# A decode block's backward pass: some weight loads and gradient stores move from SyncE's DMA queue to GpSimd's

## The chip, the cores and the metric

The kernel runs on one core of one Trainium2 chip. The metric is device time in microseconds (us) of one execution; the figure for a kernel is the median over several. A core has five engines with a queue of instructions each: TensorE (PE, with its weight loads shown apart as PEld), VectorE (DVE), ScalarE (ACT), GpSimd (POOL) and SyncE (SP). Memory traffic is carried by 16 DMA engines, which the profile shows by queue and packet. Any of SP, ACT and POOL can issue a DMA; the instruction that does so stands in that engine's own queue, in order with its other work.

## The reference, cut to what matters

One decode step (one token, batch 2) through attention and a gated MLP side by side, and then the gradients of everything. The forward part is

```
xn  = layernorm(x)                                  # x: 2 x 1 x 576
q   = xn @ wq                                       # wq: 576 x 4096, 32 heads of 128
p   = softmax(q k^T / sqrt(128));  o = p v          # k, v: 2 x 16 x 4096 x 128, two q heads share one kv head
out = x + o @ wo + ((xn @ w_gate) * (xn @ w_up)) @ w_down   # wo: 4096 x 576; F = 4608
```

and what is returned is `out` and the gradients for x, the k cache, the v cache, wq, wo, w_gate, w_up and w_down, all in bf16. The gradients of the caches are as large as the caches, those of the weights as large as the weights. With one token for each of two batch rows every weight gradient is an outer product of rank 2, and every cache gradient one of rank 2 (two q heads). So nearly every byte is either read once or written once: 92.48 MB in, 92.48 MB out.

## The kernel before, in words

**Tiles and stages.** Attention is worked in 16 steps (s): 8 groups g of two kv heads, and for each the two batch rows. A step loads two K tiles and two V tiles of 1 MB (128 partitions x 8 KB, `load_kv`, L1044), turns each by 32x32 blocks on VectorE (`turn`, L1113), makes scores on TensorE (`score`, L1162), the softmax (`softmax`, L1211), contracts with V and K (`contract`, L1335), and writes two dK and two dV tiles of 1 MB as outer products (`head_outer`, L1183), which go through PSUM, are copied to a `big` buffer by ScalarE or VectorE (`cp`, L461 and L463) and stored. The blocks `BD` that the outer products need are built by GpSimd, 3.6 us each (`build_BD`, L1150); so are the small stationaries `W` (`build_W`, L1127) and `wt` (`stationaries`, L661).

A group has a front (`group_front`: q from wq, the gradient of o from wo) and a back (`group_back`, L957: the gradients of that group's 512 columns of wq and 512 rows of wo, its share of the output and of dx). The MLP runs in 9 slices of 512 columns (`mlp`) between the steps.

**What is loaded and stored for a group.** `load_w` (L1050) loads a group's wq as 128 partitions x 4 runs of 1,024 bytes (L1063, 512 KB), with two small loads of 32 KB for the last 64 rows (L1059), and wo as 128 partitions x 4 runs of 1,152 bytes (L1068, 576 KB). The four runs of a partition lie together in SBUF and apart in memory. In `group_back` the gradient of wo goes out as 4,608-byte runs (`rows_outer`, 576 KB), the main part of wq's gradient as 1,024-byte runs (`cols_outer` with `cols_store`, L732, 512 KB), and the last 64 rows of wq's gradient as one 64 KB store (`tail_outer`, L759, buffer `tl`). The MLP's weights and gradients use the same helpers with runs of 2,048 bytes.

**What sets the order.** Each piece of work is a generator. A planner written out in the kernel (`Order`, L105) runs them when the program is built: each request has an engine, a cost, and a priority from tables (`PR`, `HEAD`, `TAIL`, `OFF`, with a step of 28 a step); the planner keeps a model of when engines and buffers come free and of two DMA lines (`Lines`, L53), one for SP and ACT and one for POOL, and emits instructions in the order it arrives at. On the chip each engine then runs its own instructions in exactly that order. A DMA is costed at L291: a packet of `row` bytes takes 0.0364 ns a byte and 8.7 ns more. `SLACK` says how far ahead of the earliest candidate an engine may look for one of higher priority. `load_ws` (L1097) holds each weight load until so many cache loads have been issued (`MLP_AT`, `WQ_AT`, `WO_AT`).

**Queues.** In this kernel all loads and stores are issued by SP, but for the two loads of x and grad_out (ACT). `put` (L677) is the one helper for stores: it waits for the copies that fill the buffer and issues on SP. POOL issues no DMA.

The functions that the change touches, and what calls them:

Of the kernel before, what the change touches and what calls it, by code (L numbers as in the profile page):

```python
# [13 lines left out]
P = 128  # L14
# [276 lines left out]
def DMA(engine, cost, nbytes, row=8192):  # L291
    packet = 0.0364 * row + 8.7
    return ("dma", engine, cost, 0.02 + nbytes / 16e3 * packet / row, packet)
# [2 lines left out]

NBIG, NGU, NWW, NBD = 16, 1, 6, 3
CAP = {"kv": 7, "X": 12, "st": 4, "G": 2}
OFF = {"mload": {0: -36.3, 1: 16.8, 2: -19.8, 3: -330.5, 5: 42.4, 6: -111.1, 7: -82.2, 9: 191.7, 10: -151.2,
       11: 244.5, 13: -16.7, 15: -5.8}, "wload": {0: 329.7, 1: -827.0, 2: -91.1, 3: 193.0, 4: -575.9, 5: 77.0,  # L300
       6: -97.7, 7: 317.9, 8: 179.1, 10: 110.7, 11: 107.3, 12: 101.9, 13: 558.1, 14: -92.8, 15: 306.7},
       "BD1": {0: 482.2, 1: -53.2, 2: -3.3, 3: 120.6, 4: -601.2, 5: -133.1, 6: 127.1, 7: -234.1, 8: -45.0, 9: 65.6,
       10: 99.4, 12: -193.8, 13: 284.9, 14: -109.9, 15: 42.6}, "out1": {0: 49.6, 1: 283.1, 2: 49.7, 3: -222.7,
       5: 323.4, 6: 229.4, 7: -322.6, 8: 142.3, 9: 293.7, 10: 4.2, 11: 63.5, 12: -219.7, 13: -100.2, 14: 383.8,
       15: 47.0}, "W1": {0: -170.8, 1: -216.4, 2: -400.0, 3: -75.8, 4: -98.4, 5: 118.6, 6: 303.1, 7: 8.0, 9: 60.0,
       10: -3.6, 11: -275.6, 12: -452.3, 13: 182.8, 14: -7.3, 15: 237.8}, "turn1": {0: -195.1, 1: -56.4, 2: -119.7,
       3: 124.4, 4: 468.7, 6: -73.7, 7: 79.5, 8: -132.5, 9: -229.3, 10: -53.9, 11: 85.0, 12: 1.5, 14: -33.0,
       15: 38.8}, "load": {0: 38.1, 1: -50.7, 2: 166.0, 4: -99.4, 5: -145.2, 6: -9.7, 7: 192.6, 8: -2.7, 9: 97.8,
       10: -119.3, 12: 290.3, 13: -19.5, 14: -128.7, 15: 181.9}, "front": {0: 9.1, 1: 170.2, 2: 128.1, 3: 372.2,
       4: 357.2, 5: -384.9, 6: -177.7, 7: -129.0, 8: 13.5, 9: 71.0, 10: 224.9, 11: 9.5, 12: -117.9, 13: -9.4,  # L310
       14: -468.5, 15: -30.4}, "turn0": {0: -455.2, 1: -90.8, 2: 0.2, 3: 28.7, 4: -0.9, 5: -231.7, 6: 2.8, 7: 67.0,
       8: -476.7, 9: 30.4, 10: -61.0, 11: 29.9, 12: 6.4, 13: -275.6, 14: 105.2, 15: 86.1}, "con": {0: 60.0, 1: 31.3,
       2: 117.9, 3: -65.0, 4: 446.2, 5: 4.0, 6: -193.2, 7: -1.9, 8: 27.1, 9: -358.4, 10: 38.5, 11: -215.9, 12: -87.1,
       13: 7.6, 15: 22.9}, "W0": {0: -4.4, 1: 75.7, 2: -298.1, 3: 59.6, 4: 289.8, 5: -179.5, 6: 58.5, 7: -263.0,
       8: -20.6, 9: 21.9, 12: 520.5, 13: -109.7, 14: -223.2, 15: -36.8}, "back": {0: -320.5, 1: 0.4, 2: 125.7,
       3: 144.8, 4: -34.1, 5: 27.8, 6: -144.7, 7: -3.0, 8: -92.9, 9: -20.3, 10: -85.3, 11: -52.0, 13: 82.4,
       14: -138.2}, "BD0": {0: 13.0, 1: -92.4, 2: 161.5, 3: -159.8, 4: -155.8, 6: -113.5, 7: -55.4, 9: 148.4,
       10: 97.8, 11: 7.0, 12: -22.3, 13: 117.7, 14: 473.8, 15: 16.2}, "out0": {0: -47.5, 1: -241.0, 2: 70.9,
       3: -176.7, 4: -156.5, 5: -403.1, 7: 101.3, 8: -9.1, 9: -258.5, 10: 100.0, 11: -93.4, 12: 255.6, 13: -226.2,
       14: -11.9, 15: -60.8}, "dsc": {0: -366.7, 2: 10.9, 3: 185.9, 5: -2.6, 7: 31.8, 8: -250.0, 9: 24.5, 10: 26.4,  # L320
       12: -2.1, 13: -284.2, 14: 187.2, 15: -38.2}, "mlp": {0: -345.4, 2: 692.3, 3: -3.8, 4: -34.2, 5: 612.9,
       6: 368.1, 7: -119.8, 8: 31.4, 10: -111.7, 11: -100.0, 12: 51.0, 13: 219.8, 14: 9.4, 15: 136.1},
       "att": {0: -32.2, 1: 181.3, 2: 325.2, 3: 101.2, 4: 36.6, 5: 184.0, 6: -133.3, 7: -37.0, 8: 57.4, 9: 139.5,
       10: -6.1, 11: -267.5, 12: 36.3, 13: -80.2, 14: -101.6}, "conv": {0: -191.0, 1: -570.3, 2: 91.8, 3: 215.3,
       4: 4.9, 5: 4.5, 6: 46.9, 7: -237.0, 8: 83.3, 9: -6.7, 10: -56.4, 11: -31.6, 13: -155.6, 14: -88.6, 15: -378.3}}
MLP_AT = [2.38, 3.44, 16.76, 17.06, 29.05, 44.32, 47.73, 43.88, 59.6]
WQ_AT = [-3, 9, 17, 23, 32, 39, 50, 55]
WO_AT = [2, 7, 5, 25, 36, 39, 37, 57]
LATENCY, DRY = {"SP": 0.5, "ACT": 0.5, "POOL": 0.57}, 0.4
LM, LAG = 0.15, 1.75  # L330
CLK = 2.0
BIAS = 0.547
SLACK = {"PE": 0.08, "ACT": 0.3, "DVE": 0.46, "POOL": 24.94, "SP": 1554.58}
STEP = 28.0
HEAD = {"turn0": 358.0, "turn1": -88.8, "att": -420.1, "dsc": 372.9, "con": 241.2, "out1": -625.8, "out0": 80.7,
        "front": 43.6, "back": 73.0, "W0": 584.4, "W1": -340.9, "BD1": 39.3, "BD0": 397.4, "conv": 284.3,
        "load": 102.5}
TAIL = {"turn0": 773.4, "turn1": 743.4, "att": -103.0, "dsc": 772.1, "con": 784.6, "conv": 1032.9, "out1": 1117.1,
        "out0": 440.4, "front": -1213.5, "back": 298.4, "W1": 286.6, "BD1": 566.8, "BD0": -240.2, "load": 315.8,
        "W0": 700.2}  # L340
PR = {"turn0": 179.4, "turn1": -212.5, "att": -999.3, "dsc": -1293.8, "conv": 102.1, "con": -320.2, "out1": 2170.9,
      "out0": 547.6, "front": 160.8, "back": -141.3, "W0": -800.5, "W1": -140.0, "BD1": 814.6, "BD0": -99.0,
      "mlp": -127.6, "wout": -665.8, "store": 229.4, "load": 79.4, "wload": -1000.4, "fin": -292.2, "const": 321.0,
      "mload": -108.2}


def pr(name, s):
# [5 lines left out]
def kernel(  # L353
# [22 lines left out]
    nc = tc.nc  # L376
# [297 lines left out]
                                 rhs=view(Xt, 0, P, toff(q, s), [[2, 32]]),  # L674
                                 start=(s == 0), stop=(s == St - 1))

    def put(dst, src, nbytes, row, tag, slot, ready):  # L677
        yield WAIT(*ready)
        for d, x in zip(dst, src):
            yield DMA("SP", 0.36, nbytes, row)  # L680
            nc.sync.dma_start(d, x)
        yield ("lrel", tag, slot)

    def unit(mms, pe, cols, ev, done, quad=None, kind="r"):
# [44 lines left out]
        yield WAIT(*done)  # L729
        yield SET(event)  # L730

    def cols_store(i, dst, width, done):  # L732
        return put([dst.rearrange("(c p) n -> p c n", p=P)], [st_t[i][:, 0:4 * width].rearrange("p (c n) -> p c n", n=width)],
                   128 * 4 * width * 2, 2 * width, "st", i, done)

    def cols_outer(rhs, dst, p, event):
        i = yield ACQ("st")
        done = events(2)
        yield SPAWN(cols_store(i, dst, FS, done), p + PR["store"])
        for A in range(2):  # L740
            yield SPAWN(unit(*cols_unit(A, rhs, st_t[i]), done[A]), p)
        yield WAIT(*done)
        yield SET(event)
# [12 lines left out]
        yield WAIT(*done)  # L756
        yield SET(event)

    def tail_outer(rhss, dsts, p, event):  # L759
        i = yield ACQ("tl")  # L760
        st = tl_t[i]
        nw, done = len(rhss), events(2)
        yield SPAWN(put(dsts, [st[64 * w:64 * w + 64, 0:FS] for w in range(nw)], 64 * FS * 2, 1024, "tl", i, done),
                    p + PR["store"])

        def mk(A):
            def mms(o):
                for w, rhs in enumerate(rhss):
                    for aa in range(2):
                        a = 2 * A + aa  # L770
                        nc.tensor.matmul(o[64 * w:64 * w + 64, aa, 0:P], lhsT=xnr[32 * a:32 * a + 32, 512:576],
                                         rhs=rhs(a), start=True, stop=True)

            def ev(e, o):
                cp(e, st[0:64 * nw, 256 * A:256 * A + 256].rearrange("p (a f) -> p a f", a=2), o[0:64 * nw, :, 0:P])
            return mms, (0.053, 0.104), 256, ev
        for A in range(2):
            yield SPAWN(unit(*mk(A), done[A]), p)
        yield WAIT(*done)
        yield SET(event)  # L780
# [176 lines left out]
    def group_back(g):  # L957
# [16 lines left out]
        po = pr("back", 2 * g) + PR["wout"]  # L974
        yield SPAWN(rows_outer(R[:], out_5[n0:n0 + FS, :], po, E[0]), po)
        yield SPAWN(cols_outer(lambda a: R[32 * a:32 * a + 32, 1, :], out_4[0:512, n0:n0 + FS], po, E[1]), po)
        yield SPAWN(tail_outer([lambda a: R[32 * a:32 * a + 32, 1, :]], [out_4[512:576, n0:n0 + FS]], po, E[2]), po)
        m = yield ACQ("m")
        yp = m_t[m][:, 0:10].rearrange("p (k b) -> p k b", b=2)
        yield PE(0.0, 0.52)  # L980
# [69 lines left out]
    def load_w(item):  # L1050
        kind, i = item
        if kind in ("wq", "wo"):
# [3 lines left out]
            if kind == "wq":  # L1056
                for h in range(2):
# [1 line left out]
                    nc.sync.dma_start(ww_t[w][64 * h:64 * h + 64, 4 * FS:WB],  # L1059
                                      A_wq[512:576, n0 + 256 * h:n0 + 256 * h + 256])  # L1060
                yield ("lset", st["Lq"])
                yield DMA("SP", 0.4, 128 * 4 * FS * 2, 1024)
                nc.sync.dma_start(ww_t[w][:, 0:4 * FS].rearrange("p (c n) -> p c n", n=FS),  # L1063
                                    A_wq[0:512, n0:n0 + FS].rearrange("(c p) n -> p c n", p=P))
                yield ("lset", st["Lm"])
            else:
                yield DMA("SP", 0.4, 128 * GH * D * 2, 1152)
                nc.sync.dma_start(ww_t[w][:, 0:GH * D].rearrange("p (h n) -> p h n", h=GH),  # L1068
                                  A_wo[n0:n0 + FS, :].rearrange("(h p) n -> p h n", p=P))
                yield ("lset", st["Lo"])  # L1070
        else:
# [419 lines left out]
```

## Time and profile before

| | |
|---|---|
| median of 3 runs | 482.09 us (481.51 to 482.98) |
| the profiled execution's own time | 483.47 us |
| its span, first to last instruction | 481.7 us (1.8 us lie around it) |
| mean granted TensorE clock | 0.675 |
| busy: PE, PEld, DVE, ACT, POOL | 386.8, 217.9, 360.0, 343.2, 155.4 us |
| moved by DMA | 185.94 MB, mean 386 GB/s |

How to read it: busy times are of the engine itself; time in which its queue waits or issues a DMA is not counted. The page's second part cuts the span into 40 slices of 12 us, each digit a busy share in tenths; the row "DMA" is the mean busy share of the 16 DMA engines, and "GB/s" what they moved. A DMA answer for a short window counts the packets that start in it, by size class, and gives the time those packets took as a share of 16 engines over the window; packets run over the window's end, and so a full second can show a little over 100%. A packet here is one run of bytes (1,024, 1,152, 2,048, 4,608 or 8,192) or a 4-byte completion. The DMA instruction lasts only as long as its issue; "us to landing" is counted from there to the arrival of its data.

### The profile page before, as it was taken

What the parts mean: (1) busy time and instruction counts of PE and PEld (TensorE: products, weight loads), DVE (VectorE), ACT (ScalarE), POOL (GpSimd) and SP (SyncE); (2) the same over time, 40 slices, a digit from 0 to 9 for tenths busy, and PEclk for the clock granted to TensorE, in tenths of its full rate; (3) what the DMA queues carried; (4) which work ended last, traced back from release to release, by engine and by line L of the source; (5) the groups of instructions that cost most, each with busy time, mean ns of one, the idle gap of its engine ahead of it and who ended that gap; (6) DMA issues with size and microseconds to landing.
All of it is one profiled execution on the core that took longest, in us unless ns stands there. A gap on an engine that the chain in (4) does not pass through costs nothing.

```text
span 481.7 us, 15312 instructions
## 1 busy us (share of the span) xinstructions
PE 386.8 (80%) x6530; PEld 217.9 (45%) x6530; DVE 360.0 (75%) x667; ACT 343.2 (71%) x520; POOL 155.4 (32%) x220
## 2 busy tenths in 40 slices
PE   1479699858788878868977899857698899899897
PEld 1456345435444444434654345324465434554444
DVE  8688877867377977776677778866665988788872
ACT  6066578956787596755598779856578877868883
POOL 3110553443011374320026364361102724074100
PEclk9995657669656578677786557756965555765765
DMA  7997999999999999999999999999999999999994
GB/s 289 353 406 269 367 387 386 401 343 399 424 406 417 390 416 420 365 399 407 415 406 417 342 407 422 424 403 388 413 386 411 420 326 403 419 395 419 405 412 163
DMA packets 49652, 185.94 MB, mean 386 GB/s; under 512 B 4008, under 2 KB 21168, under 8 KB 33200
## 3 DMA queue, kind: packets, MB, share of 16 engines
q1 hardware_dynamic: 49576, 184.96, 98.0%
q8 instruction: 51, 0.84, 0.7%
q14 instruction: 17, 0.14, 0.1%
q10 hardware_dynamic: 8, 0.00, 0.0%
HBM read 92.48 MB, written 92.48 MB: 384 GB/s over the span
## 4 chain that ended last, share of the span: by engine, by line
DMA 46%; PE 30%; ACT 10%; DVE 7%; issue 4%; SPq 3%; DVEq 0%; ACTq 0%
DMA out_dram<-big 29%; ACT big L461 8%; PE ps_o L1183 6%; PE ps_m L1335 5%; DMA big<-in_A_k_cache_dram 5%; DMA big<-in_A_v_cache_dram 5%; PE ps_m L1162 4%; DVE big L457 3%; DMA ww<-in_B_w_down_dram 3%; PE ps_o L715 3%; DMA ww<-in_A_wo_dram 2%; PE ps_m L941 2%; DVE big L463 2%; DMA ww<-in_A_wq_dram 1%; PE ps_o L701 1%
## 5 line engine op out<-in xcount | busy, mean ns | idle before, releaser
L461 ACT CAST big<-ps_o 128x1024 bf16<-128x1024 f32 (+1 forms) x319 | 283.0, 955 | 41.0 <-PE ps_o L1183 22.1
L457 DVE STREAM_TRANSPOSE big<-big 128x1024 f32<-128x1024 f32 x146 | 175.8, 1223 | 23.9 <-DMA out_dram<-big 17.0
L1150 POOL TENSOR_TENSOR BD<-vr,mask 128x2048 bf16<-128x2048 bf16 x32 | 115.3, 3602 | 114.1 <-PE ps_o L1183 40.8
L463 DVE CAST big<-ps_o 128x1024 bf16<-128x1024 f32 (+1 forms) x57 | 66.4, 1166 | 12.8 <-PE ps_o L1183 4.3
L1162 PE MATMUL ps_m<-big,W 128*32 128x128 bf16 x2048 | 60.4, 286 | 4.2 <-POOL W L1127 1.3
L1162 PEld LDWEIGHTS <-W 128*32 128x32 bf16 x2048 | 47.8, 127 | 22.4 <-issue 19.3
L1183 PE MATMUL ps_o<-BD,dd 32*128 32x512 bf16 x256 | 51.4, 527 | 7.5 <-ACT big L461 5.5
L1183 PE MATMUL ps_o<-BD,pp 32*128 32x512 bf16 x256 | 47.6, 520 | 8.4 <-ACT big L461 6.4
L1127 POOL COPY W<-rep 32x16 bf16<-32x16 bf16 x128 | 24.5, 192 | 69.9 <-DVE rep L925 65.0
L661 POOL COPY wt<-wm 64x128 bf16<-64x128 bf16 (+1 forms) x34 | 8.9, 261 | 99.2 <-DVE wm L654 98.3
L457 DVE STREAM_TRANSPOSE big<-ww 128x1152 f32<-128x1152 f32 x25 | 34.1, 1365 | 7.5 <-DMA out_dram<-big 4.8
L1335 PE MATMUL ps_m<-big,dd 128*32 128x512 bf16 x256 | 28.8, 540 | 9.8 <-DVE dd L457 4.7
L1335 PE MATMUL ps_m<-big,pp 128*32 128x512 bf16 x256 | 30.2, 566 | 1.4 <-DVE pp L457 0.9
L1183 PEld LDWEIGHTS <-dd 32*128 32x128 bf16 x256 | 12.0, 98 | 30.6 <-issue 26.5
L1183 PEld LDWEIGHTS <-pp 32*128 32x128 bf16 x256 | 11.0, 98 | 24.7 <-issue 21.1
L701 PEld LDWEIGHTS <-xnr 32*128 32x128 bf16 x416 | 13.7, 110 | 14.4 <-issue 12.9
L715 PE MATMUL ps_o<-dyr,R 32*32 32x288 bf16 x256 | 18.1, 396 | 2.1 <-ACT big L461 1.1
L461 ACT CAST osb<-ps_m 128x512 bf16<-128x512 f32 x16 | 9.6, 598 | 12.7 <-PE ps_m L1335 9.3
L941 PE MATMUL ps_m<-big,Wdy 128*128 128x128 bf16 x144 | 15.4, 292 | 3.4 <-DVE cr L1287 1.8
L701 PE MATMUL ps_o<-hb,xnr 32*128 32x128 bf16 x288 | 14.3, 250 | 4.5 <-ACT big L461 3.2
L715 PE MATMUL ps_o<-dyr,hb 32*32 32x288 bf16 x288 | 16.1, 337 | 1.1 <-DVE tl L463 0.5
L941 PEld LDWEIGHTS <-Wdy 128*128 128x128 bf16 x144 | 13.8, 134 | 6.3 <-issue 6.3
(198 smaller groups left out, 486.6 us busy)
## 6 DMA issues: line engine op xcount, KB each, us to landing
out_dram<-big SPq DMA_DIRECT2D x72, 1024.0 KB, 12.2
big<-in_A_k_cache_dram SPq DMA_DIRECT2D x32, 1024.0 KB, 11.5
big<-in_A_v_cache_dram SPq DMA_DIRECT2D x32, 1024.0 KB, 13.1
out_dram<-big SPq DMA_DIRECT2D x17, 576.0 KB, 10.8
ww<-in_B_w_down_dram SPq DMA_DIRECT2D x9, 576.0 KB, 12.4
out_dram<-big SPq DMA_DIRECT2D x10, 512.0 KB, 9.6
ww<-in_A_wo_dram SPq DMA_DIRECT2D x8, 576.0 KB, 12.3
ww<-in_A_wq_dram SPq DMA_DIRECT2D x8, 512.0 KB, 9.7
```

Of the source, the lines that this page charges most:

```text
L457: nc.vector.transpose(out, in_)
L461: nc.scalar.copy(out, in_)
L463: nc.vector.tensor_copy(out=out, in_=in_)
L661: nc.gpsimd.tensor_copy(view(Wt[:], 64 * h, 64, 0, [[dims[-1][1], n], [1, dims[-1][1]]]), view(Wm[:], 64 * h, 64, off, dims))
L701: nc.tensor.matmul(o[:, aa, dc * P:(dc + 1) * P], lhsT=xnr[32 * a:32 * a + 32, dc * P:(dc + 1) * P], rhs=rhs(a), start=True, stop=True)
L715: nc.tensor.matmul(o[32 * q:32 * q + 32, aa, 0:HD2], lhsT=view(t, 32 * q, 32, 2 * A + aa, [[4, 32]]), rhs=dyr[32 * q:32 * q + 32, k * HD2: ...
L941: nc.tensor.matmul(dp, lhsT=Wdy[:, e, 2 * k:2 * k + P], rhs=view(X[:], 0, P, 64 * k + e, [[D, GH], [2, 32]]), start=(k == 0 and e == 0), s ...
L1127: nc.gpsimd.tensor_copy(view(W_t[t][w][:], 32 * a, 32, 6 + 8 * a, [[G * WW, 4], [WW, G], [1, 2]]), view(rep_t[grp[g]["qs"]][:], 32 * a, 32 ...
L1150: nc.gpsimd.tensor_tensor(BD_t[i][:], view(vr_t[v][:], 0, P, 0, [[0, 16], [1, Dh]]), view(mask16[:], 0, P, 0, [[1, 16], [0, Dh]]), ALU.mult)
L1162: nc.tensor.matmul(sc[32 * cq:32 * cq + 32, :], lhsT=view(W[:], 0, P, (be * G + l) * WW + 6 - 4 * c2 - 2 * l, [[1, 32]]), rhs=view(X[:], 0 ...
L1183: nc.tensor.matmul(o[:, k, :], lhsT=pr2[32 * c4:32 * c4 + 32, :], rhs=BD[32 * c4:32 * c4 + 32, 8 * l + 4 * h2:8 * l + 4 * h2 + 4, :], star ...
L1335: nc.tensor.matmul(ct[32 * j:32 * j + 32, :], lhsT=view(rT, 0, P, 4 * c + 2 * l, [[1, 32]]), rhs=kv_t[kvS[s][t][l]][:, Dh * c:Dh * (c + 4) ...
```

## The change

What it does: (1) `put` and `cols_store` get an `engine` argument; with "POOL" the DMA is issued by GpSimd. (2) `cols_outer`, which stores the main part of wq's gradient, uses it: 8 stores of 512 KB. (3) In `load_w`, from the second group on, the main load of wq (7 of 512 KB) and the load of wo (7 of 576 KB) are issued by GpSimd. In the planner's books these 22 DMAs cost the issuing engine 0.78 us (0.36 or 0.4 on SP) and count as rows of 4,096 or 4,608 bytes, four times as long as before. (4) `tail_outer` gets `w0`: the 64 rows of a group's wq tail use partitions 0 to 63 for even groups and 64 to 127 for odd ones. (5) All tables of the planner have other values: the priorities, the gates, two landing delays, the bias between ACT and DVE for copies, and `SLACK`. No arithmetic is added or removed.

```
-MLP_AT = [2.38, 3.44, 16.76, 17.06, 29.05, 44.32, 47.73, 43.88, 59.6]
-WQ_AT = [-3, 9, 17, 23, 32, 39, 50, 55]
-WO_AT = [2, 7, 5, 25, 36, 39, 37, 57]
+MLP_AT = [2.82, 10.88, 15.0, 36.18, 28.54, 28.05, 46.37, 36.8, 60.65]
+WQ_AT = [-6, 9, 17, 24, 32, 29, 48, 55]
+WO_AT = [2, -2, -17, 15, 35, 39, 40, 53]
...
-LM, LAG = 0.15, 1.75
+LM, LAG = 1.27, 1.14
...
-BIAS = 0.547
-SLACK = {"PE": 0.08, "ACT": 0.3, "DVE": 0.46, "POOL": 24.94, "SP": 1554.58}
+BIAS = 0.599
+SLACK = {"PE": 0.04, "ACT": 0.27, "DVE": 0.45, "POOL": 1.44, "SP": 13.16}
...
-    def put(dst, src, nbytes, row, tag, slot, ready):
+    def put(dst, src, nbytes, row, tag, slot, ready, engine="SP"):
         yield WAIT(*ready)
         for d, x in zip(dst, src):
-            yield DMA("SP", 0.36, nbytes, row)
-            nc.sync.dma_start(d, x)
+            yield DMA(engine, 0.36 if engine == "SP" else 0.78, nbytes, row)
+            (nc.sync if engine == "SP" else nc.gpsimd).dma_start(d, x)
...
-    def cols_store(i, dst, width, done):
+    def cols_store(i, dst, width, done, engine="SP"):
...
-                   128 * 4 * width * 2, 2 * width, "st", i, done)
+                   128 * 4 * width * 2, 2 * width if engine == "SP" else 8 * width, "st", i, done, engine)
...
-        yield SPAWN(cols_store(i, dst, FS, done), p + PR["store"])
+        yield SPAWN(cols_store(i, dst, FS, done, "POOL"), p + PR["store"])
...
-    def tail_outer(rhss, dsts, p, event):
+    def tail_outer(rhss, dsts, p, event, w0=0):
...
-        yield SPAWN(put(dsts, [st[64 * w:64 * w + 64, 0:FS] for w in range(nw)], 64 * FS * 2, 1024, "tl", i, done),
+        yield SPAWN(put(dsts, [st[64 * w:64 * w + 64, 0:FS] for w in range(w0, w0 + nw)], 64 * FS * 2, 1024, "tl", i, done),
...
-        yield SPAWN(tail_outer([lambda a: R[32 * a:32 * a + 32, 1, :]], [out_4[512:576, n0:n0 + FS]], po, E[2]), po)
+        yield SPAWN(tail_outer([lambda a: R[32 * a:32 * a + 32, 1, :]], [out_4[512:576, n0:n0 + FS]], po, E[2], g % 2), po)
...
-                yield DMA("SP", 0.4, 128 * 4 * FS * 2, 1024)
-                nc.sync.dma_start(ww_t[w][:, 0:4 * FS].rearrange("p (c n) -> p c n", n=FS),
+                yield DMA("POOL", 0.78, 128 * 4 * FS * 2, 4096) if i else DMA("SP", 0.4, 128 * 4 * FS * 2, 1024)
+                (nc.gpsimd if i else nc.sync).dma_start(ww_t[w][:, 0:4 * FS].rearrange("p (c n) -> p c n", n=FS),
...
-                yield DMA("SP", 0.4, 128 * GH * D * 2, 1152)
-                nc.sync.dma_start(ww_t[w][:, 0:GH * D].rearrange("p (h n) -> p h n", h=GH),
+                yield DMA("POOL", 0.78, 128 * GH * D * 2, 4608) if i else DMA("SP", 0.4, 128 * GH * D * 2, 1152)
+                (nc.gpsimd if i else nc.sync).dma_start(ww_t[w][:, 0:GH * D].rearrange("p (h n) -> p h n", h=GH),
```

## The prediction

> **What bounds the kernel now.** I read the page's first three parts first. Its busy row, DMA row and queue table:
>
> ```profile
> PE 386.8 (80%) x6530; PEld 217.9 (45%) x6530; DVE 360.0 (75%) x667; ACT 343.2 (71%) x520; POOL 155.4 (32%) x220
> ...
> DMA  7997999999999999999999999999999999999994
> ...
> DMA packets 49652, 185.94 MB, mean 386 GB/s; under 512 B 4008, under 2 KB 21168, under 8 KB 33200
> ...
> q1 hardware_dynamic: 49576, 184.96, 98.0%
> ```
>
> No compute engine is over 80% busy, while the packets of one DMA queue, q1 (SP's), take 98.0% of the time of all 16 DMA engines. Under 90% the DMA row shows only the first slice, the fourth and the last. So the time is that of the packets, plus the little in which the DMA engines starve. The chain of waits says the same: 46% of it are DMA, and PE comes only second.
>
> Next I asked for the stages, cut where the DMA row dips (columns: window and its length; busy time of PE, PEld, DVE, ACT, POOL; granted clock; DMA share; GB/s):
>
> ```profile
> 0.00:4.00 4.00, 0.00 (x0) 0.00 (x0) 3.10 (x10) 2.35 (x5) 3.39 (x17) 1.00 0.21 50
> 34.00:41.00 7.00, 5.89 (x131) 3.63 (x128) 6.99 (x14) 3.56 (x5) 0.29 (x1) 0.57 0.54 172
> 41.00:386.00 345.00, 280.56 (x4849) 158.46 (x4847) 256.02 (x446) 254.29 (x387) 122.86 (x155) 0.66 1.02 399
> 386.00:393.00 7.00, 6.39 (x80) 2.29 (x69) 5.88 (x12) 5.31 (x9) 1.76 (x1) 0.50 0.84 307
> 470.00:481.70 11.70, 8.23 (x87) 4.94 (x84) 3.23 (x13) 3.76 (x6) 0.00 (x0) 0.50 0.41 155
> ```
>
> For 345 us on end the DMA engines are full. They starve for 4.0 x 0.79 = 3.2 us at the start, 7.0 x 0.46 = 3.2 us at 34 to 41 us (the first gradients aren't ready and the cache buffers are all taken), 7.0 x 0.16 = 1.1 us at 386 to 393, and 11.7 x 0.59 = 6.9 us at the end. A full DMA engine that moves 399 GB/s where windows of 8 KB packets alone move 426 loses to small packets. What one packet of a kind costs I took from DMA answers for windows that hold almost one kind only. The two most used here, of 1,024 bytes (456 to 457 us) and 8,192 bytes (236 to 240 us):
>
> ```profile
> DMA packets 349, 0.38 MB, mean 381 GB/s; under 512 B 12, under 2 KB 342, under 8 KB 346
> q1 hardware_dynamic: 349, 0.38, 106.7%
> ```
>
> ```profile
> DMA packets 228, 1.70 MB, mean 426 GB/s; under 512 B 20, under 2 KB 20, under 8 KB 20
> q1 hardware_dynamic: 228, 1.70, 100.9%
> ```
>
> The second: 208 packets in 1.009 x 16 x 4 = 64.6 us, 310 ns each. The first: 106.7% of 16 engine-microseconds are 17.1; 4 packets of 2 to 8 KB and 3 of 8 KB take about 1.7, and 15.4 us for 330 packets is 46.7 ns each. In the same way 1,152 bytes (13 to 14 us: 106.3%, 327 packets and one of 8 KB) come to 51.0 ns, 2,048 bytes (47 to 50 us: 104.5%, 588) to 85.3, 4,608 bytes (23 to 24 us: 99.8%, 88) to 181. Per kilobyte the short ones cost 46, the long ones 39 to 40 ns.
>
> **The change, part by part. The packets.** 15 transfers of 512 KB (7 loads of wq, 8 stores of its gradient) are 7,680 runs of 1,024 bytes, 7 of 576 KB (wo) are 3,584 runs of 1,152. The diff counts them as rows of 4,096 and 4,608 bytes, that is, one packet for the four runs of a partition. No row shows a packet of GpSimd's queue, so I bound it. Dear end: packets stay as they are, nothing saved (the bytes and runs are the same, so the engines have no more to carry). Cheap end: the diff's rows are true. A 4,096-byte packet lies between the 2,048 and 4,608 rows at 85.3 + (181 - 85.3) x 0.8 = 162 ns; four short ones are 187. 1,920 times 25 ns over 16 engines: 3.0 us. For wo, four at 51.0 are 204 against 181; 896 times 23 ns over 16: 1.3 us. Together **-4.3 us**. All of it is on the path, since the DMA engines are full in the stages where these transfers lie. I take the cheap end: four runs that lie together in a partition's SBUF are the only thing that sets these transfers apart, and the 4,608-byte row shows that an engine takes such a length as one packet.
>
> The Trainium skill ("DMA: Bandwidth & Descriptors", section "Why small descriptors are slow") puts a packet's fixed cost at about 3 cycles and says that joining is worth it only up to 256 bytes. By its 3 cycles at 850 MHz, 3.5 ns, I estimate 2,816 x 3 x 3.5 / 16 = 1.8 us in place of 4.3. The rows above disagree: 46.7 ns against a fourth of 162, 40.5, is 6 ns a run. The sum stays with the rows.
>
> **SP's queue** loses 22 issues of about 0.5 us (medians of the two load lines: 0.58 and 0.48), 11 us in all, and the waits for the eight gradient stores' copies. SP isn't the bound, since its DMAs take 8 to 15 us to land in a full queue: nothing. What was queued behind those waits, cache loads above all, can go out sooner; it joins a full line.
>
> **GpSimd's queue** gains 22 issues and eight waits for copies. No row shows the price of an issue there: at SP's 0.58 us it is 13 us, at GpSimd's own longest instruction, 3.6 us, it is 79, on 155.4 busy of 481.7. I take 0.58, the same transfer's row. The cover is GpSimd's slack: its BD blocks, asked by line, held up PE for 0.3 us and its weight loads for 0.5 in the whole run. At 79 us each issue would delay a BD block by about one block, once in 22 us; the DMA engines would notice only if stores then ran dry, which is the second rival.
>
> ```profile
> L1150 POOL TENSOR_TENSOR BD<-vr,mask x32: 3601/3602/3605, 49.1 to 443.5; 128x2048 bf16<-128x2048 bf16 x32
> ```
>
> The BD line by source (min, median, max ns) shows GpSimd's longest work undisturbed by a VectorE that is 75% busy: 4 ns between fastest and slowest of 32. That bears on a rule against this change. The Trainium skill ("SBUF — State Buffer", the box on VectorE blocking DMA) says that GpSimd writes the descriptors of its DMAs itself and is locked out while VectorE runs a two-port copy; a 620 ns transfer then took 3,100. By that I estimate 22 x 2.5 = 55 us more on GpSimd, which lies within the two ends above; no run here shows a descriptor being written.
>
> **The tails** move the same 26 stores of 64 KB, with the same packets, from other partitions: nothing. If the half mattered, eight stores of 64 packets at 46.7 ns over 16 engines are 1.5 us in all, and a part of that could be won or lost.
>
> **The tables** change the order everywhere. That moves starving, not packets: at best the stretch at 34 to 41 us closes (-3.2 us; the start and the last step's chain have nothing to load or store), at worst new ones open (second rival). I take nothing.
>
> **Sum:** 483.47 - 4.3 = 479.2 us on the profiled execution's clock. That execution is 1.4 us over the median of 482.09; so 482.09 - 4.3 = **477.8 us**. With the 34 to 41 us stretch closed it is 474.6; with half the saving, about 480.
>
> **Rivals.** *No saving.* GpSimd's queue makes the same packets, and everything else was hidden anyway: 482.1 us. For it: only the diff's own numbers say that runs are joined. The Trainium skill ("DMA: Bandwidth & Descriptors", section "Issuing engines are not separate DMA queues") has this rule: whichever engine issues, the same 16 engines carry it, and only issue time is saved. The first half the trace can't show with one queue; by it alone the time stays. Against it: the change of packet length, which that rule doesn't speak of.
>
> *GpSimd's queue blocks, and the DMA engines starve.* On GpSimd a load or store stands in order behind waits, and BD blocks stand behind its own waits. The waits by engine:
>
> ```profile
> POOL wt L661 <- DVE wm L654: 98.3, 16, 21.1
> POOL W L1127 <- DVE rep L925: 65.0, 14, 15.9
> POOL BD L1150 <- PE ps_o L1183: 40.8, 6, 11.2
> ```
>
> (us in all, times, longest.) A wo load behind a wait of 11 to 21 us lands late; the group's front then waits, and after it scores, outer products and stores. Against it: loads wait for a gate long before they are needed, and wq and wo held up their users for 4.0 and 1.3 us in all. It costs nothing until stores in flight run out; then one starving is worth what 34 to 41 us shows, 3.2 us. Two undo the gain, so it decides from the second on. I price three, in seven groups: 482.1 - 4.3 + 9.7 = **487.5 us**, slower.
>
> **How the numbers follow.** Forecast 0.56; no saving 0.14; blocking 0.30. About 0.3%, 1.4 us, is what a measurement of this kernel can tell from no change. So faster 0.56, same 0.14, slower 0.30. The likeliest case's own range is 474.6 to 480.5. The range must also take in the no-saving case and most of the blocking one: 474.6 to 487.5 us.
>
> **What would show it.** A second queue in the queue table with 7.9 + 4.1 = 12.0 MB, 2,816 packets of 4 KB and more beside its completions, and q1 short of 11,264 packets: "under 2 KB" falls from 21,168 to about 9,900. If the second queue shows 11,264 packets, the first rival holds. The DMA share in the middle stage stays at 1.0 and GB/s rises from 399 by some 4. If GpSimd blocks, PE's waits for BD rise from 0.3 us to tens, and the DMA row shows new digits under 9. GpSimd's issues by line give their price; over 3.6 us my cover is wrong. The forecast fails if two queues at once slow each other's packets: 8 KB packets would then take more than 310 ns while GpSimd's transfers are in flight.

## The result, and the profile after

| | time, us | ratio to before, 95% interval |
|---|---|---|
| before | 482.83, median of 15 runs (481.51 to 484.66) | |
| after | 484.72, median of 15 runs (482.78 to 487.91) | 1.0052 (1.0030 to 1.0074) |

The change makes the kernel slower by 0.5%, where 1% faster was forecast. The profiled execution of after took 487.82 us, 3.1 over its median, span 485.8. From its page: busy row, DMA row, packets, and the queue table (packets, MB, share of 16 engines' time):

```profile
PE 383.6 (79%) x6530; PEld 218.8 (45%) x6530; DVE 353.4 (73%) x661; ACT 348.2 (72%) x526; POOL 172.6 (36%) x242
...
DMA  7997999999999999999999999999999999999994
...
DMA packets 41204, 185.94 MB, mean 383 GB/s; under 512 B 4008, under 2 KB 9904, under 8 KB 24752
...
q1 hardware_dynamic: 37960, 172.97, 90.8%
q0 software_dynamic: 3168, 11.99, 6.5%
```

The marks that the forecast named for the packets are there. A second queue, q0, carries 11.99 MB in 3,168 packets: 352 completions and 2,816 packets of 4 KB and more, so the four runs of a partition are one packet. "Under 2 KB" falls from 21,168 to 9,904. The two queues together take 97.3% of the engines' time where one took 98.0%. The mark for the rate is missing: in the long full stretch (columns as in the prediction; DMA share and GB/s last) the engines move 398 GB/s, where before moved 399 and some 4 more were forecast.

```profile
88.00:428.00 340.00, 279.60 (x4736) 157.19 (x4724) 251.06 (x443) 260.22 (x394) 137.87 (x178) 0.66 1.01 398
```

So the packets changed as forecast and the time didn't follow.

GpSimd's new issues, by line (the store, the wq load, the wo load; ns min, median, max):

```profile
L682 POOL DMA_DIRECT2D out_dram<-big x8: 759/800/800, 86.1 to 477.6; - x8
```

```profile
L1065 POOL DMA_DIRECT2D ww<-in_A_wq_dram x7: 751/792/920, 53.8 to 387.5; - x7
L1070 POOL DMA_DIRECT2D ww<-in_A_wo_dram x7: 751/751/792, 54.8 to 388.3; - x7
```

0.75 to 0.92 us each, 17 us in all, which is the rise of POOL's busy time from 155.4 to 172.6: on GpSimd, unlike on SP, the profile counts an issue as busy. PE waited for BD blocks 1.1 us in the whole run (0.3 before): GpSimd was not short of time.

### The profile page after: what moved, and what is told of

Same layout as the page of the kernel before. It is cut to its first block, busy times and chain, and to the rows that moved or that the text cites. A ratio compares the mean times of both kernels' runs of the same rounds, so it can differ in the third digit from the quotient of the medians.

```text
span 485.8 us, 15354 instructions
## 1 busy us (share of the span) xinstructions
PE 383.6 (79%) x6530; PEld 218.8 (45%) x6530; DVE 353.4 (73%) x661; ACT 348.2 (72%) x526; POOL 172.6 (36%) x242
## 3 DMA queue, kind: packets, MB, share of 16 engines
q0 software_dynamic: 3168, 11.99, 6.5%
## 4 chain that ended last, share of the span: by engine, by line
DMA 40%; PE 32%; ACT 12%; DVE 10%; issue 3%; POOL 1%; SPq 0%; DVEq 0%; ACTq 0%; POOLq 0%
DMA out_dram<-big 22%; ACT big L462 10%; DMA big<-in_B_w_gate_dram 6%; PE ps_o L1185 5%; PE ps_o L716 5%; DVE big L458 5%; DMA big<-in_A_v_cache_dram 5%; PE ps_m L1337 4%; PE ps_m L1164 4%; DMA gu<-in_B_w_up_dram 3%; PE ps_m L943 2%; DMA ww<-in_A_wq_dram 2%; DMA big<-in_A_k_cache_dram 2%; DVE big L464 2%; PE ps_o L702 2%
## 5 line engine op out<-in xcount | busy, mean ns | idle before, releaser
L462 ACT CAST big<-ps_o 128x1024 bf16<-128x1024 f32 (+1 forms) x324 | 287.5, 952 | 43.8 <-PE ps_o L1185 27.2
L464 DVE CAST big<-ps_o 128x1024 bf16<-128x1024 f32 (+1 forms) x52 | 60.7, 1170 | 10.3 <-PE ps_o L1185 3.5
L1185 PE MATMUL ps_o<-BD,pp 32*128 32x512 bf16 x256 | 50.3, 521 | 10.8 <-ACT big L462 8.4
L1185 PE MATMUL ps_o<-BD,dd 32*128 32x512 bf16 x256 | 45.5, 491 | 8.6 <-ACT big L462 5.4
L1337 PE MATMUL ps_m<-big,pp 128*32 128x512 bf16 x256 | 31.7, 583 | 3.6 <-DVE pp L458 2.5
L1337 PE MATMUL ps_m<-big,dd 128*32 128x512 bf16 x256 | 26.8, 510 | 1.7 <-DVE oT L1357 1.4
L1185 PEld LDWEIGHTS <-dd 32*128 32x128 bf16 x256 | 10.7, 97 | 29.3 <-issue 24.5
L716 PE MATMUL ps_o<-dyr,hb 32*32 32x288 bf16 x288 | 18.8, 383 | 3.6 <-DVE tl L464 3.0
L716 PE MATMUL ps_o<-dyr,R 32*32 32x288 bf16 x256 | 19.2, 431 | 1.4 <-ACT big L462 1.4
L462 ACT CAST osb<-ps_m 128x512 bf16<-128x512 f32 x16 | 9.4, 589 | 13.1 <-PE ps_m L1337 9.2
L669 PE MATMUL ps_m<-big,wm 128*32 128x128 bf16 x416 | 13.3, 286 | 7.0 <-DVE hb L809 3.2
```

What stands on the lines that cost most here:

```text
L462: nc.scalar.copy(out, in_)
L464: nc.vector.tensor_copy(out=out, in_=in_)
L669: nc.tensor.matmul(dp[32 * q:32 * q + 32, 0:P], lhsT=view(Wm[:], 0, P, 8 * pos(q, s), [[1, 32]]), rhs=view(X, 0, P, xoff(q, s), [[xstep, 4 ...
L716: nc.tensor.matmul(o[32 * q:32 * q + 32, aa, 0:HD2], lhsT=view(t, 32 * q, 32, 2 * A + aa, [[4, 32]]), rhs=dyr[32 * q:32 * q + 32, k * HD2: ...
L1185: nc.tensor.matmul(o[:, k, :], lhsT=pr2[32 * c4:32 * c4 + 32, :], rhs=BD[32 * c4:32 * c4 + 32, 8 * l + 4 * h2:8 * l + 4 * h2 + 4, :], star ...
L1337: nc.tensor.matmul(ct[32 * j:32 * j + 32, :], lhsT=view(rT, 0, P, 4 * c + 2 * l, [[1, 32]]), rhs=kv_t[kvS[s][t][l]][:, Dh * c:Dh * (c + 4) ...
```

## The experiments

All times are medians; ratios are to the kernel before, run on the same chip. Two theories at the start. "Order": the second queue saves the forecast 4 us, and the order that comes out of the new tables costs more than that. "Queue": the second queue itself costs.

### The queue and the order apart

Since the order is fixed when the program is built, the issuing engine can be changed without touching the order of PE, DVE and ACT: the planner keeps its books, and only the call goes to another engine.

**b_pool**, before's order, GpSimd issues the 22 transfers:

```
             yield DMA("SP", 0.36, nbytes, row)
-            nc.sync.dma_start(d, x)
+            (eng or nc.sync).dma_start(d, x)      # eng = nc.gpsimd from cols_outer
...
-                nc.sync.dma_start(ww_t[w][:, 0:4 * FS]...
+                (nc.gpsimd if i else nc.sync).dma_start(ww_t[w][:, 0:4 * FS]...   # wo alike
```

> The kernel before, instruction by instruction in the order of before on PE, DVE, ACT; only the engine that issues the 22 main transfers is GpSimd. Theory 'order' (the second queue saves packet time as forecast, the new tables cost it back): about 4 us faster than before, ratio 0.990 to 0.994, the share of q0 and q1 together down by some 4 us of the span. Theory 'queue' (two queues at once slow each other's packets, or GpSimd's order blocks): 484 us or more, ratio 1.002 to 1.01, mean GB/s of the full stages not above before's.

**a_sp**, after's order and halves, all issued by SP:

```
-                (nc.gpsimd if i else nc.sync).dma_start(...)
+                nc.sync.dma_start(...)                # wq, wo, and in put
```

> The changed kernel, order of after on PE, DVE, ACT, the tails on changed halves; but SP issues the 22 transfers. Theory 'order': the packets' saving is lost on top, about 488 to 490 us, ratio to before 1.012 to 1.016. Theory 'queue': the loss goes with the queue, about 481 to 484 us, ratio 0.997 to 1.002.

**a_code_b_tables** and **b_code_a_tables**: the block of tables exchanged, from `OFF` to `PR`, the rest as in after and in before.

> The changed code with the tables of before: the planner knows of GpSimd's queue but has the old priorities. The order comes out new from the planner. Theory 'order': near before less the packets, 477 to 481 us, unless the new order starves by chance. Theory 'queue': 484 us or more.

> The code of before with the new tables: all on SP's queue, planner's books for SP. Theory 'order': 487 us or more, ratio 1.01 or more. Theory 'queue': within 0.3% of before, since the tables alone do no harm.

| kernel | time, us | ratio (95%) |
|---|---|---|
| b_pool | 487.55 | 1.0101 (1.0075 to 1.0127) |
| a_sp | 484.92 | 1.0056 (1.0031 to 1.0080) |
| after, for comparison | 484.72 | 1.0052 (1.0030 to 1.0074) |
| a_code_b_tables | 507.79 | 1.0527 (1.0500 to 1.0554) |
| b_code_a_tables | 500.96 | 1.0389 (1.0363 to 1.0415) |

Neither theory stands as it was put. On before's order the queue alone costs 1.0%; so it doesn't save 4 us ("order" falls). On after's order taking the queue away changes nothing, 1.0056 against 1.0052, intervals nearly the same; so the loss doesn't go with the queue either ("queue" falls). What the two share is that the packets' saving is seen in neither. The exchanged tables told nothing about the queue: each set of priorities is bound to one set of the planner's books, and with the other the end of the run starves (in b_code_a_tables the DMA share is 0.73 from 440 us on). In a_code_b_tables the last 68 us, by stage (the last two columns are DMA share and GB/s):

```profile
440.00:508.00 68.00, 53.33 (x764) 28.16 (x764) 38.10 (x69) 48.29 (x69) 14.99 (x12) 0.58 0.77 308
```

A DMA share of 0.77 there; these two runs measure the tables' fit and nothing else.

### Where before's order loses by the queue

In the trace of b_pool, PE's timeline at 56 to 63 us, with the idle time and who ended it in brackets:

```profile
56.63 0.59 PE L1246 MATMUL ps_m<-z,G 128*128 128x1 f32 x2
62.06 0.69 PE L908 MATMUL ps_m<-xs,ww 128*128 128x2 bf16 x20 [4.84 <-DMA ww<-in_A_wq_dram]
```

and the same place before:

```profile
57.60 0.59 PE L1246 MATMUL ps_m<-z,G 128*128 128x1 f32 x2
60.15 0.69 PE L908 MATMUL ps_m<-xs,ww 128*128 128x2 bf16 x20 [1.96 <-DMA ww<-in_A_wq_dram]
```

PE executes in order, and the front of the second group stands at the head of its queue, waiting for wq. On SP's queue that wq was issued at 53.60 us and PE went on at 60.15, 6.5 us later; on GpSimd's it was issued at 51.66 and PE went on at 62.06, 10.4 us later. The records of the packets split the longer way. On SP the first packet of this wq started 2.1 us after the issue, and the last ended 4.0 us after that; on GpSimd it was 4.1 us to the first packet and 5.4 us from there to the last. So about 2 us go by before the first packet, and some 1.4 us more while a line of its own shares the engines with the 1 MB transfers of q1, here at 56 to 61 us in b_pool:

```profile
q1 hardware_dynamic: 167, 0.90, 49.8%
q0 software_dynamic: 218, 0.88, 47.1%
```

Why the first packet comes late isn't shown. GpSimd's and VectorE's other work isn't needed for it: in the probes below, which compute nothing, the first packet of GpSimd's queue came 4.6 us after its issue beside busy engines (probe_pool) and 1.6 us after it on idle ones (probe_small_pool).

PE comes out 1.9 us later, and the stores behind it too. The DMA engines then starve at 63 to 69 us, by 6 x 0.39 = 2.3 us (before, the share there was 0.99):

```profile
63.00:69.00 6.00, 5.87 (x103) 2.86 (x99) 4.77 (x9) 5.40 (x8) 1.76 (x1) 0.69 0.61 253
```

This gave a new pair of theories, "sharing" and "blocking", for three runs, all in before's order: **b_pool_store** (only the eight stores on GpSimd), **b_pool_load** (only the 14 loads), and **b_pool_g2** (all but the second group's wq and wo: `if i` becomes `if i > 1`).

> The kernel before in its own order; only the eight 512 KB gradient stores are issued by GpSimd. Theory 'sharing' (a load on a second queue shares the engines packet by packet with the 1 MB transfers, lands later where it is wanted at once, and the PE queue then stands still): stores hold up nobody, so 0 to 2 us faster than before (1,024 packets of 4 KB, some 25 ns each over 16 engines: 1.6 us less), ratio 0.996 to 1.000. Theory 'blocking' (GpSimd stands behind the copies that a store waits for, and BD blocks come late): 2 to 5 us slower, ratio 1.004 to 1.010.

> The kernel before in its own order; only the 14 weight loads from the second group on are issued by GpSimd. Theory 'sharing': the whole loss of the run with all 22, 485 to 488 us, ratio 1.005 to 1.011. Theory 'blocking': a load waits for little on GpSimd, so within 0.3% of before.

> As the run with all 22 transfers on GpSimd in the order of before, but the second group's wq and wo stay on SP, where wq was wanted at once. Theory 'sharing': PE no longer stands 4.8 us at 57 to 62 us, 2 to 3 us of the loss come back: 484 to 486 us, ratio 1.003 to 1.007. If the loss is made elsewhere: 487 to 488 us as with all 22.

| kernel | time, us | ratio (95%) |
|---|---|---|
| b_pool_store | 483.73 | 1.0017 (1.0000 to 1.0034) |
| b_pool_load | 485.35 | 1.0039 (1.0012 to 1.0065) |
| b_pool_g2 | 484.16 | 1.0038 (1.0022 to 1.0054) |

Putting one group's two loads back on SP brings 1.0101 down to 1.0038, about 3 us, and its trace shows the gain at that place: PE waits for wq 2.56 us where it waited 4.84, and the DMA share at 63 to 69 us is 0.96 where it was 0.61.

```profile
59.59 0.69 PE L908 MATMUL ps_m<-xs,ww 128*128 128x2 bf16 x20 [2.56 <-DMA ww<-in_A_wq_dram]
63.00:69.00 6.00, 6.00 (x71) 2.41 (x69) 4.31 (x10) 4.57 (x7) 3.90 (x3) 0.50 0.96 373
```

So some 3 of the 5 us are lost by the late landing of these two loads, as "sharing" had it; that the larger part of the delay lies before the first packet is something the theory didn't name. The stores alone cost little or nothing, and save nothing. The loads alone cost 1.0039, less than "sharing" expected (1.005 to 1.011), though the interval reaches into that. The parts don't add up to 1.0101; stores and loads together make it worse than either, and by what isn't shown (b_pool ran on another chip than the other three, each against before on its own chip).

### What joined packets are worth

These runs compute nothing: they only move data, 64 cache tiles of 1 MB in and out on SP, and between them 64 weight loads (wq and wo in turn) and 32 gradient stores of 512 KB in short rows, on the queue under test. The other outputs stay unwritten.

```
+ for n in range(64):                    # few = nc.sync, nc.gpsimd, nc.scalar or none
+     few.dma_start(ww_t[n % 8]..., A_wq or A_wo ...)        # as L1063, L1068
+     nc.sync.dma_start(kv_t[n % 12][:], views[t][b, h])
+ for n in range(64):
+     if n % 2 == 0: few.dma_start(out_4[0:512, ...], kv_t[n % 12][:, 0:4 * FS]...)
+     nc.sync.dma_start(oviews[t][b, h], kv_t[n % 12][:])
```

**probe_sp** and, on another chip with the next two, **probe_sp2**: all on SP.

> Computes nothing: loads all 64 cache tiles of 1 MB on SP with 32 wq and 32 wo main loads between them on SP, then stores 64 tiles of 1 MB with 32 stores of 512 KB in rows of 1,024 bytes between them; the other outputs stay unwritten. By the single-packet prices: 131,072 packets... of 8 KB are 32,768 x 310 / 16 = 635... that is 64 + 64 tiles at 20.3 us of one engine's line each 2.54 us: 325 us; 64 transfers of 512 KB at 1.49 us and 32 of 576 KB at 1.63 us: 148 us; about 473 us if packets of one queue do not overlap, some 10 us less if the 3% above 100% seen in windows of short packets is real overlap.

> The probe on SP alone once more, beside the other two on the same chip: 469 to 472 us.

**probe_pool**: the 96 short-row transfers on GpSimd.

> Computes nothing: the transfers of the probe on SP alone (64 cache tiles of 1 MB in and out, 64 weight loads of 512 and 576 KB, 32 stores of 512 KB), but the 96 short-row transfers are issued by GpSimd. By the forecast's prices (25 ns for each 4 KB of 1,024-byte rows: 128 x 25 / 16 = 0.20 us a transfer of wq or of its gradient; 23 ns for each 4,608 bytes: 0.18 us for wo) 64 x 0.20 + 32 x 0.18 = 18.6 us less than the probe on SP, about 452 us. If short packets of one queue overlap, so that their recorded time is not what they cost, 5 to 10 us less, 460 to 466 us. If two queues at once slow each other's packets: no gain or a loss, 470 us or more.

**probe_none**: without them.

> Computes nothing: only the 64 loads and 64 stores of 1 MB on SP, no short rows. 65,536 packets... 128 transfers of 1 MB are 16,384 packets of 8 KB, at 310 ns over 16 engines 317 us, and some 8 us at both ends. It gives by difference what the 96 short-row transfers cost on either queue: 471 - 325 = 146 us, 1.5 us each, on SP.

**probe_act**: the 96 on ACT. **probe_all_pool**: everything on GpSimd. **probe_small_sp**, **probe_small_pool**: the 96 alone, without the 1 MB tiles (the stores then read `ww`). These four ran on a third chip.

> Computes nothing: the probe with its 96 short-row transfers on ACT's queue, so a second queue, but rows of 1,024 and 1,152 bytes as on SP. Theory 'interleave' (joined rows do save their 18 us, and two queues at once cost as much again): the second queue costs without a saving, 480 to 487 us against 468.7 on SP alone. Theory 'no price' (a packet's recorded time overlaps its neighbour's, so that the bytes set the time and joining saves nothing): 467 to 472 us.

> Computes nothing: the whole probe on GpSimd's queue, 1 MB tiles too, so one queue with joined rows. Theory 'interleave': 450 to 456 us, the 18 us are there. Theory 'no price': 467 to 473 us. More than that would say that GpSimd cannot issue 224 transfers fast enough or that its 1 MB transfers cost more.

> Computes nothing: only the 96 short-row transfers (52.4 MB) on SP. By the difference of the probes, 1.52 us each: 146 us and 4 to 6 us at the ends, 150 to 153 us.

> Computes nothing: only the 96 short-row transfers, on GpSimd alone. Theory 'interleave': 64 x 1.30 + 32 x 1.45 = 130 us and the ends, 134 to 137 us. Theory 'no price': as on SP, 149 to 154 us.

| kernel | time, us | each short-row transfer, by difference to probe_none |
|---|---|---|
| probe_none | 322.53 | |
| probe_sp, probe_sp2 | 470.62, 468.67 | (468.67 - 322.53) / 96 = 1.52 us |
| probe_act (second queue, short packets) | 470.23 | 1.54 us |
| probe_pool (second queue, joined packets) | 471.53 | 1.55 us |
| probe_all_pool (one queue, joined packets) | 481.49 | |
| probe_small_sp (short packets) | 150.43 | |
| probe_small_pool (joined packets) | 154.82 | |

(The first figures in probe_sp's and probe_none's expectations are slips of the pen; the sums after them are what was expected.) The forecast's prices gave 452 us for probe_pool, 450 to 456 for probe_all_pool and 134 to 137 for probe_small_pool. None came near. A second queue with short packets costs next to nothing: probe_act lies 1.6 us over probe_sp2, but on another chip, and the same kernel on two chips (probe_sp, probe_sp2) differs by 2.0. So "interleave" falls. Joining shows no gain in company or alone, as "no price" said, though two of its times were missed: probe_small_pool is just over the 149 to 154 us, and probe_all_pool 8 us over the 467 to 473. Why there is no gain is seen in the stretch 60 to 90 us of the two small probes. On SP:

```profile
DMA packets 10500, 11.09 MB, mean 370 GB/s; under 512 B 319, under 2 KB 10500, under 8 KB 10500
q1 hardware_dynamic: 10500, 11.09, 109.4%
```

On GpSimd:

```profile
DMA packets 2865, 11.04 MB, mean 368 GB/s; under 512 B 319, under 2 KB 319, under 8 KB 2864
q0 software_dynamic: 2864, 11.03, 103.1%
```

A fourth of the packets, the same bytes in the same 30 us. 10,181 short packets took 109.4% of the engines' time, 51.6 ns each; that more than 100% is recorded means that they lie one over another. The 2,545 joined ones took 103.1%: 1.031 x 16 x 30 us, less the completions, is 193 ns each where 162 to 181 had been priced. A packet's recorded time is so no price that can be summed: the joined packet gets longer and the overlap smaller, until the rate is the same. By the packets' records both probes needed 54.4 us from the 10th to the 30th megabyte. What probe_small_pool takes longer lies in its start and in its stores (328 GB/s at 120 to 140 us, 341 on SP).

Joining and GpSimd's queue change together in these probes: no run has joined packets on SP's queue, or short ones on GpSimd's. A saving that GpSimd's queue takes back exactly is therefore not excluded. That the loads run level in both pairs, 368 against 370 GB/s here and 402 against 402 below, makes it unlikely.

Beside the 1 MB tiles it is their packets that get longer. In probe_pool, 60 to 250 us:

```profile
DMA packets 13715, 76.42 MB, mean 402 GB/s; under 512 B 1529, under 2 KB 1529, under 8 KB 7622
q1 hardware_dynamic: 6858, 49.91, 66.3%
q0 software_dynamic: 6856, 26.51, 35.6%
```

q1 there has 6,092 packets of 8 KB (49.91 MB) in 0.663 x 16 x 190 us: 330 ns each, against 313 in probe_none (100.1% of 16 x 320.6 us for 16,384). Beside ACT's queue of short packets they stay at 314 (probe_act, the same window, 404 GB/s), so it isn't a second queue as such that lengthens them. On SP alone the same window moves 76.39 MB, 402 GB/s too:

```profile
DMA packets 31845, 76.39 MB, mean 402 GB/s; under 512 B 1517, under 2 KB 25735, under 8 KB 25735
q1 hardware_dynamic: 31844, 76.38, 104.1%
```

probe_all_pool took 10 to 13 us longer than the others; it is slower than either theory had it. GpSimd was busy for 29% of its span, so it wasn't out of issue time. Its loads are level with the others (402 GB/s at 60 to 250 us); the loss lies in the stores (391 GB/s at 300 to 440 us, 400 in probe_sp2), the last few megabytes above all. Why GpSimd's queue is slower there stays open.

### The order and the halves apart

With the queue worth nothing on the new order, the 0.5% lies in the order or in the tails' halves. **b_tail**: before with `w0 = g % 2`, every engine's order unchanged. **a_sp_notail**: after's order, all on SP, tails on partitions 0 to 63.

> The kernel before, every engine's order unchanged, all on SP; only the wq tails of odd groups use partitions 64 to 127. If the halves do nothing, as forecast: within 0.3% of before. If they matter, by at most the 1.5 us that the eight stores take.

> The changed kernel's order on PE, DVE and ACT, but SP issues everything and the tails stay on partitions 0 to 63: the new tables' order alone. If the order alone makes the loss: ratio to before 1.003 to 1.008, as the changed kernel. If the halves made it: within 0.3% of before.

b_tail took 483.44 us, ratio 1.0003 (0.9983 to 1.0023): the halves do nothing that these runs can tell. a_sp_notail took 485.83 us, ratio 1.0065 (1.0045 to 1.0085): the order alone makes the loss, within the intervals the whole of it. Two stretches where the new order starves the engines (DMA share and GB/s last), first before, then a_sp_notail, then after:

```profile
80.00:90.00 10.00, 8.88 (x115) 4.23 (x118) 9.49 (x15) 9.42 (x16) 2.55 (x11) 0.64 1.01 412
290.00:302.00 12.00, 11.48 (x188) 6.64 (x185) 10.41 (x18) 11.18 (x20) 5.53 (x10) 0.78 1.01 425
```

```profile
80.00:90.00 10.00, 7.77 (x109) 4.01 (x101) 8.00 (x17) 8.37 (x15) 5.36 (x8) 0.67 0.85 327
290.00:302.00 12.00, 9.20 (x143) 5.55 (x145) 11.12 (x20) 10.30 (x15) 4.96 (x8) 0.73 0.74 280
```

```profile
80.00:90.00 10.00, 8.27 (x139) 4.98 (x137) 6.61 (x16) 7.93 (x14) 4.04 (x4) 0.67 0.79 309
290.00:302.00 12.00, 10.15 (x159) 4.66 (x161) 11.05 (x18) 8.54 (x12) 5.49 (x10) 0.65 0.99 397
```

At 80 to 90 us the new order starves the engines, by 10 x 0.15 = 1.5 us on SP and 10 x 0.21 = 2.1 us with the queue; before, they were full. SP's timeline in after shows how:

```profile
74.98 1.11 SPq L1046 DMA_DIRECT2D big<-in_A_v_cache_dram  x1
84.04 0.34 SPq L682 DMA_DIRECT2D out_dram<-big  x1
85.59 0.50 SPq L682 DMA_DIRECT2D out_dram<-tl  x1
86.94 3.59 SPq L682 DMA_DIRECT2D out_dram<-big  x2
90.62 0.44 SPq L1046 DMA_DIRECT2D big<-in_A_v_cache_dram  x1
```

Between 76.1 and 84.0 us SP issues nothing: a store whose copies aren't done stands at the head, and the next cache load comes only at 90.62. Before, SP stood there just as long, but had more in the line:

```profile
71.63 0.34 SPq L681 DMA_DIRECT2D out_dram<-big  x1
72.08 0.38 SPq L1044 DMA_DIRECT2D big<-in_A_k_cache_dram  x1
72.50 0.43 SPq L1044 DMA_DIRECT2D big<-in_A_v_cache_dram  x1
75.79 8.65 SPq L681 DMA_DIRECT2D out_dram<-big  x2
```

From 62 to 76 us SP issued four cache loads and four stores before, and four cache loads and three stores in after; the store at 75.79 is the one more.

At 290 to 302 us the new order starves on SP (12 x 0.26 = 3.1 us) and hardly with the queue. GpSimd's queue moves nothing in that window, q1 takes 98.9%; it helped ahead of it. A wo load went out at 276.62 us on SP, right behind two cache loads, and at 276.88 on GpSimd. VectorE stood waiting for it, first in a_sp_notail, then in after:

```profile
289.74 1.38 DVE L458 STREAM_TRANSPOSE big<-ww 128x1152 f32<-128x1152 f32 x1 [4.45 <-DMA ww<-in_A_wo_dram]
286.65 1.38 DVE L458 STREAM_TRANSPOSE big<-ww 128x1152 f32<-128x1152 f32 x1 [1.34 <-DMA ww<-in_A_wo_dram]
```

So here the load was in use 9.8 us after its issue on the second queue, and 13.1 us after it on SP's. That the stretch starves for this reason is likely, and no run of its own shows it. It is the one place where the second queue was seen to help, and over the run it is worth no more than it loses elsewhere.

The two stretches show where new starving opened; they don't add up to the 0.65%. The executions traced lasted nearly the same, 483.47 us (before) and 484.04 (a_sp_notail, the fastest of its 12; after's, at 487.82, is near its slowest). And the new order also closes starving that before had at 386 to 393 us (0.84) and at the end (0.41). In a_sp_notail:

```profile
386.00:393.00 7.00, 6.55 (x121) 3.70 (x113) 6.12 (x12) 6.68 (x9) 0.00 (x0) 0.57 1.02 385
470.00:482.00 12.00, 8.25 (x87) 4.95 (x84) 3.16 (x13) 3.76 (x6) 0.00 (x0) 0.50 0.55 213
```

That the order costs 0.65% is shown by the medians; which stretches make it up in a median execution is not.

## Why the prediction was wrong

*Bound by DMA:* right. The engines are full in after as before, and the losses that could be placed lie where they starve.

*The packets, -4.3 us:* **the step that failed.** The text took the cheap end: joined rows, at 162 ns for 4,096 bytes, "all of it is on the path". The first half was right. The packets were joined, 2,816 of them, and their recorded time was near the price: q0's 6.5% of 16 x 485.8 us, less the completions, is 178 ns each, where the two prices average 168. The second half was wrong, since recorded time saved is not time saved: the probes show 1.55 us for a transfer on GpSimd's queue against 1.52 on SP's, and on the new order the kernel takes as long with the queue as without it (1.0052, 1.0056). In place of -4.3 us stands nothing. The error is in the method. I divided a window's recorded time by its packets and used the quotient as a cost. The windows that gave the prices showed 106.7 and 106.3%, which I put down to packets running over a window's end; a whole 30 us at 109.4% can't be that. What could be compared from the trace of before was the rate: window by window, bytes moved, not time recorded. It would have promised less, though not nothing: 381 and 385 GB/s in the windows of short rows against 406 in that of 4,608 bytes make, as an estimate, 1.8 us on 12.0 MB. No window of before holds rows that are joined on one side and apart in memory.

*The 1.8 us by the 3 cycles a packet* of the Trainium skill ("DMA: Bandwidth & Descriptors", section "Why small descriptors are slow"): nearer than the rows, and still not there; no gain was measured.

*SP's queue, nothing:* not as put. The 11 us of issue time show no worth (a_sp, where SP keeps them, takes as long as after), but what stood in SP's line mattered, to wq in b_pool and to wo at 277 us.

*GpSimd's issue, 0.58 us, hidden:* 0.75 to 0.92, hidden. Of the rule that VectorE locks GpSimd out of descriptor writing (the Trainium skill, "SBUF — State Buffer", the box on VectorE blocking DMA) the issues show no sign: 0.75 to 0.92 us with VectorE 73% busy, and 0.75 (L418, L421 and L431 of probe_pool, 72.3 us for the 96 and four memsets) with VectorE idle. Whether VectorE ran any copy of the kind that the rule names, no run shows.

*The tails, nothing:* right as far as it can be told (1.0003).

*The tables, nothing taken:* the second term that failed, and the one that gives the result its sign: +0.65% by themselves, about 3 us. The stretch at 34 to 41 us did not close, and a new one opened at 82 to 88. With nothing for the packets and the 0.56 to 0.65% of a_sp and a_sp_notail for the order, the sum would be 484.8 to 485.2 us.

*"No saving":* it was right that nothing is saved, and half wrong in its reason: not the same packets, but the same rate. Its time, 482.1, lacks the order's loss. The rule beside it, that the same 16 engines carry the data whoever issues (the Trainium skill, "DMA: Bandwidth & Descriptors", section "Issuing engines are not separate DMA queues"), agrees with 468.7, 470.2 and 471.5 us for the short rows from SP, ACT and GpSimd; the 481.5 us of probe_all_pool stay unexplained beside it.

*"Blocking":* the kernel came out slower, as it said, but its mechanism wasn't seen. PE's waits for BD blocks rose to 1.1 us, not to tens. GpSimd's queue wasn't what stood; where the queue cost (b_pool), PE stood, for a load that had left early and landed late.

The last sign named, 8 KB packets over 310 ns beside GpSimd's transfers, did appear (330 ns in probe_pool), at an unchanged rate: a recorded time once more, and not a cost.

The range of 474.6 to 487.5 holds the 484.72 by luck: its upper end was the price of blocking, and what made the time, the order, had no term in it.

## What to carry to other kernels

When the DMA engines are full, price a change of packets by the rate of whole stretches (bytes moved in a stretch with such packets and without), never by summing recorded packet times: a stretch recorded at over 100% says that they overlap. A load that someone at the head of an in-order queue is waiting for belongs in the line where it lands first, and that has to be read from the trace: on the second queue the wq at 52 us was in use 10.4 us after its issue against 6.5 on SP's, the wo at 277 us 9.8 against 13.1. And when tables of priorities change along with a mechanism, run the mechanism on both orders: here it changed nothing on one, and cost 1.0% on the other.

## What the hardware showed that was not expected

- GpSimd's queue joins the four runs of a partition into one packet of 4,096 or 4,608 bytes; SP's queue and ACT's (probe_act) make one packet of each run.
- Loads of such rows move no faster joined on GpSimd's queue than apart on SP's: 368 against 370 GB/s alone, 402 against 402 beside 1 MB transfers. A fourth of the packets changed nothing; what keeps short rows below the 419 GB/s that 8 KB rows reach (probe_none's mean), these runs don't tell.
- Recorded packet time can exceed the engines' time by 9.4% over 30 us, for packets of 1,024 and 1,152 bytes on one queue.
- A packet of 8 KB records 313 ns alone, 314 beside ACT's queue of short packets and 330 beside GpSimd's joined ones, at 402 to 404 GB/s in the last two.
- The first packet of a second queue comes late when the engines are busy: 4.6 us after the issue on GpSimd (probe_pool) and 3.0 on ACT (probe_act), against 1.6 for GpSimd (probe_small_pool) and 1.1 for SP (probe_small_sp) on idle engines.
